# A linear-attention block and a balanced mixture of experts in one kernel: attention tiles as 64x64 products, x written behind the loads, and gathers that are issued where their lists are made

## The chip, the cores and the metric

The kernel runs on one NeuronCore of one Trainium2 chip. The metric is the device time of one execution in microseconds (us), less is better. Engines are named as the profile names them: PE is TensorE (matmuls; PEld is its weight load, which overlaps), DVE is VectorE, ACT is ScalarE, POOL is GpSimd, SP is SyncE, which here does nothing but issue DMAs. All tensors are float32.

## The reference

```
# attention, for 8 batches b and 8 heads h; seq 576, head_dim 64
kv  = einsum('bhsd,bhse->bhde', k, v)            # 64 x 64 for each head
out = einsum('bhsd,bhde->bhse', q, kv)
out = out / sqrt(mean(out*out, -1) + 1e-6) * g_norm
x   = out as (8*576, 8*64) = (4608, 512)         # a token's eight heads side by side

# mixture of experts: 8 experts, each takes exactly 4608/8 = 576 tokens
logits = x @ w_gate                              # (4608, 8)
# all 36864 logits in falling order: a token goes to the first expert that still has room
assigned = greedy_in_order(-logits, cap=576)
for e in range(8):                               # w1[e]: 512 x 1024, w2[e]: 1024 x 512
    out[assigned == e] = relu(x[assigned == e] @ w1[e]) @ w2[e]
```

## The kernel before

**Attention.** The work runs in eight slots, one for each batch. In slot `b` the kernel multiplies the tiles of batch `b` (`one`, line 464) and, between the tiles, prepares batch `b+1` (`prepare`, line 365, a generator that the slot advances by one step after each tile). Preparing a batch means: products of k and v on 64x64 quarters of the array (`sum_kv`, line 395), transposes of q (`turn_q`, line 380, into `qt`), the sum of the two halves of kv (line 417), and the gate's part: kv is transposed (line 431), copied out (`kvt`, line 433) and multiplied with `w_gate` (line 442), so that `kvx` holds for each head 64 columns of kv and 8 columns that yield the logits. A tile is 128 tokens of all 8 heads: eight products with 128 tokens as stationary columns and 72 moving columns. An even batch has four tiles; an odd one has a fifth, made of the last 64 tokens of its own and of the batch before, and that mixed tile is done as sixteen 64x64 products (line 479). Two ScalarE passes empty a tile's PSUM buffer (squares, line 485; copy to `o_sb`, line 486), VectorE sums the squares (line 490), and at the end of the slot `scale` and `logits` make the norm and the logits. GpSimd writes the normed rows to `xo` (line 511); for the last tiles (`late`) ScalarE does it instead (line 516), behind all else. Matmuls of ones (`ones`, line 361; 128x512 bf16) are put between these products: one at a slot's first tile, two at the fourth, two ahead of the kv products.

**The load queue.** All loads of q, k and v, and all writes of x to DRAM (`x_dram`), go through SP's queue in one written order, and `paced` holds each DMA until the third before it has landed. A load of batch `b+2` is issued where batch `b` has freed the buffer (`again`). The x writes wait in a list, and once it holds eight the oldest are issued at the end of a slot.

**The choice.** A chain of small DVE and PE steps (`threshold`, `assign`, `fetch`; lines 646 to 871) finds the first expert and its 576 tokens. The expert's weights are loaded, its rows of x gathered by five indirect DMAs that POOL issues (line 875), and transposed (`turn`, line 969).

**Experts.** For each expert `t`, `layers(t)` does the first layer (`one_layer`, line 1065) and the second (line 1025) by a seven-product scheme: each matrix is cut in two by two, and some of the products have a sum or difference of blocks as operand. Those sums are made on POOL: `sw` of w1's blocks (line 955, four for each of the four steps `i` of the first layer), `tw` of w2's blocks (line 1103, eight), `sh` of the hidden rows (line 1017, four after step 1 and four after the last step). The program order of POOL is kept by `in_order`: it runs its instructions in the order in which they were written. While PE works on expert `t`, the search for the next expert's tokens is fed in between (`search`, by estimated times), so that the place where the list of tokens of `t+1` (`ids`, line 869) becomes known moves from layer to layer. The gather of those rows is not put there: it waits in the list `gathers` and is written when the first layer of expert `t` has been written in full, behind the last four `sh`.

Of the kernel before, what the change touches and what calls it, by code (L numbers as in the profile page):

```python
# [7 lines left out]
FT = mybir.dt.float32  # L8
# [18 lines left out]
def kernel(  # L27
# [339 lines left out]
    def prepare(b):  # L367
# [3 lines left out]
        NT = NP * R // 2  # L371
        qt = att.tile([P, 2, NT, HP], FT, name="qt", tag="qt", bufs=3)
        turned_q[b] = qt
# [46 lines left out]

        kvx = att.tile([P, H, W], FT, name="kvx", tag="kvx", bufs=3)
        for n in range(2):
# [7 lines left out]
        for r in range(NP):  # L430
            nc.tensor.transpose(t_ps[:, r, :], kv[:, r].rearrange("p l d -> p (l d)"), ident[0:D, 0:D])
        kvt = att.tile([P, NP, D], FT, name="kvt", tag="kvt")
        nc.scalar.copy(kvt, t_ps)
        yield
# [5 lines left out]
        for r in range(NP):  # L440
            for n in range(2):
                nc.tensor.matmul(w_ps[n * D:(n + 1) * D, r], lhsT=kvt[:, r, :],
                                 rhs=gw[:, r].rearrange("p l e -> p (l e)"), start=True, stop=True)
        nc.vector.tensor_copy(kvx[:, :, D:W], w_ps.rearrange("p r (l e) -> p (r l) e", l=2))
# [3 lines left out]

    LAG = 4
    writes, late = [], []  # L450
    last_own = GC - (R + 1) // 2

    def tiles(c0, rows):
# [3 lines left out]
        o_sb = att.tile([P, T, H, W], FT, name="o_sb", tag="o_sb", bufs=2)  # L457
        xo = att.tile([P, T, H, D], FT, name="xo", tag="xo", bufs=LAG + 1)
        ms = att.tile([P, T * H], FT, name="ms", tag="ms")
# [3 lines left out]

        def one(t, copies, fill):

            o_ps = psa.tile([P, 2, 512], FT, name="o_ps", tag="o", bufs=2)
            ones(fill, o_ps[:, 0, :])
            for r2 in range(NP // 2):
                for l in range(2):
                    for rp in range(2):  # L470
                        r = 2 * r2 + rp
                        at = [slice(h * HP, (h + 1) * HP) for h in range(2)]
                        halves = rows[t]
                        parts = [(slice(0, P), halves[0], 2)] if halves[0][0] == halves[1][0] else [
                            (at[n], half, 1) for n, half in enumerate(halves)]
                        for rows_at, (bn, j), m in parts:
                            block = R * r + j
                            ks = slice(block % 2 * D, (block % 2 + 1) * D)
                            nc.tensor.matmul(  # L479
                                o_ps[rows_at, rp, (2 * r2 + l) * W:(2 * r2 + l + 1) * W],  # L480
                                lhsT=turned_q[bn][ks, l, block // 2:block // 2 + m].rearrange("p x c -> p (x c)"),
                                rhs=kv_of[bn][ks, 2 * r + l], start=True, stop=True)
            o4 = o_ps[:, :, 0:NP * W].rearrange("p b (h w) -> p b h w", w=W)
            sq = att.tile([P, H, D], FT, name="sq", tag="sq")
            nc.scalar.activation(sq.rearrange("p (b h) d -> p b h d", b=2), o4[:, :, :, 0:D], ACT.Square, scale=D ** -0.5)  # L485
            copies.append(lambda: nc.scalar.copy(o_sb[:, t].rearrange("p (b h) w -> p b (h w)", b=2), o_ps[:, :, 0:NP * W]))  # L486
            if own or t != T - 2:
                while copies:
                    copies.pop(0)()
            nc.vector.reduce_sum(out=ms[:, t * H:(t + 1) * H], in_=sq, axis=AXX)  # L490
# [38 lines left out]
    with tc.manual_schedule(engines={PE, DVE, ACTE, SPE}):  # L529
# [3 lines left out]
        for b in range(B):  # L533
# [6 lines left out]
            if b in choose_at:  # L540
                early(*choose_at[b])
            for t in range(len(rows)):
                one(t, copies, {0: 1, 3: 2}.get(t, 0))
                next(parts, None)
                if b < 2 or t == 3 or b == 6 and t == 2:
                    chore()
# [6 lines left out]
            logits()  # L553
            if b < B - 1:
                chore(2 if b == 6 else 1)

            while len(writes) >= 2 * LAG:
                writes.pop(0)()
# [245 lines left out]

    on_pool, in_second, gathers = [], set(), []

# [13 lines left out]
    def fetch(t, which, index, later):  # L820
# [50 lines left out]
        nc.vector.tensor_copy(got, s_ps[:, :, GC + 1:GC + 3])  # L871
        def gather():
            for n, (_, nr) in enumerate(blocks):
                xg = moe.tile([P, DM], FT, name="xg", tag="xg", bufs=NB)
                tokens = nc.gpsimd.indirect_dma_start(  # L875
                    out=xg[0:nr], out_offset=None, in_=x_dram,
                    in_offset=bass.IndirectOffsetOnAxis(ap=ids[0:nr, n:n + 1], axis=0))
                in_order(tokens)
                rows_of[t, n] = xg
            return tokens  # L880

        if t == 0 or t - 1 in in_second:
            tokens = gather()
        else:
            gathers.append(gather)
        if t == 0:
# [112 lines left out]
    def layers(t):  # L999
# [106 lines left out]
        yield from one_layer()  # L1106
        in_second.add(t)
        while gathers:
            gathers.pop(0)()
        for i in range(FH):  # L1110
# [138 lines left out]
```

## Time and profile before

| | us |
|---|---|
| median of 3 runs (lowest, highest) | 660.36 (658.67, 660.51) |
| the profiled execution: its own time / its span | 660.36 / 658.6 |
| attention: start of the span to the last tile's product | 0 to 121.3 |
| choice of the first expert, its loads and gather | 123 to 164 |
| experts | 164 to 657 |
| PE busy / DVE / ACT / POOL | 605.8 / 387.8 / 194.5 / 389.3 |

"Busy" sums the spans of an engine's instructions. A PE that is busy need not be at its peak: matmuls are pipelined, so that what a group of them takes is better read as the time from its start to the start of the next group. In a timeline line the first number is the start in us from the start of the span, the second the length, and a bracket at the end gives how long the engine had been idle and what ended that. In the list of waits the numbers are the total, the count, and the longest.

### The profile page before, as it was taken

The page shows a single profiled execution, that of the slowest core. Times are in us where ns is not written, and L with a number is a line of the kernel's source. Part 1 is how long each engine was busy: PE and PEld are TensorE (multiplying, and loading weights), DVE is VectorE, ACT ScalarE, POOL GpSimd, SP SyncE. Part 2 cuts the span into 40 slices and gives each one's busy share as a digit, 9 for nine tenths or more (in the row PEclk, how much of TensorE's full clock was granted, in tenths as well). Part 3 has the DMA queues.
Part 4 walks back from the last instruction along what each step waited for, and adds up shares of the span by engine and source line. Part 5 has one row for each costly group of instructions (what it writes and reads, how often), then busy time and mean ns, then how long its engine had stood idle before and what let it go on. Part 6 is the DMA issues. An engine that isn't in the chain of part 4 may idle for free.

```text
span 658.6 us, 12759 instructions
## 1 busy us (share of the span) xinstructions
PE 605.8 (92%) x4932; PEld 464.6 (71%) x4932; DVE 387.8 (59%) x1249; ACT 194.5 (30%) x395; POOL 389.3 (59%) x405
## 2 busy tenths in 40 slices
PE   7989998335899999999999999999999999999994
PEld 4767777232678677867786786778678867877873
DVE  4466667778678588668757956976671053123201
ACT  1555665611131223123212222231223123222300
POOL 1035434104585487749846974887388669848822
PEclk9999999657999999999999999999999999999998
DMA  8999989416306402710442072109103620721001
GB/s 270 310 315 295 292 291 340 154 50 199 128 0 204 164 33 71 257 41 33 158 171 73 1 262 99 41 0 323 46 32 100 229 72 1 279 84 37 0 9 64
DMA packets 49852, 91.02 MB, mean 138 GB/s; under 512 B 3712, under 2 KB 20096, under 8 KB 49792
## 3 DMA queue, kind: packets, MB, share of 16 engines
q1 hardware_dynamic: 43200, 71.31, 31.6%
q0 software_dynamic: 5888, 18.88, 8.3%
q8 instruction: 39, 0.64, 0.4%
q14 instruction: 21, 0.17, 0.1%
q10 hardware_dynamic: 704, 0.02, 0.1%
HBM read 71.32 MB, written 18.87 MB: 137 GB/s over the span
## 4 chain that ended last, share of the span: by engine, by line
PE 77%; DVE 9%; DMA 5%; issue 4%; ACT 3%; POOL 1%; POOLq 0%; SPq 0%; DVEq 0%; ACTq 0%
PE x_ps L1065 13%; PE x_ps L1025 11%; PE z_ps L1065 9%; PE y_ps L1065 9%; PE z_ps L1025 7%; PE y_ps L1025 7%; PE o_ps L479 4%; PE y_ps L1127 4%; PE kv_ps L395 3%; PE t_ps L969 3%; PE qt_ps L380 2%; DMA v_sb<-in_v_dram 2%; DMA q_sb<-in_q_dram 2%; PE given_ps L651 1%; PE given_ps L646 1%
## 5 line engine op out<-in xcount | busy, mean ns | idle before, releaser
L1070 ACT COPY h<-x_ps 128x288 f32<-128x288 f32 x93 | 37.2, 400 | 166.5 <-PE x_ps L1065 153.7
L1065 PE MATMUL x_ps<-xs,sw 128*128 128x288 f32 x248 | 71.3, 409 | 0.0
L875 POOL DMA_INDIRECT xg<-x_dram,ids x40 | 38.1, 952 | 51.8 <-DMA w_sb<-in_moe_w_dram 37.7
L992 POOL DMA_INDIRECT out_dram<-y_sb,outs x32 | 31.5, 983 | 55.8 <-DVE y_sb L1163 41.1
L1025 PE MATMUL x_ps<-tw,sh 128*128 128x256 f32 x256 | 61.6, 384 | 0.0
L972 ACT ACTIVATE xt<-t_ps,g_col 128x512 f32<-128x512 f32 (+1 forms) x40 | 25.7, 645 | 110.9 <-PE t_ps L969 110.9
L1065 PEld LDWEIGHTS x_ps<-xs,sw 128*128 128x128 f32 x248 | 46.2, 190 | 14.3 <-issue 1.7
L955 POOL TENSOR_TENSOR sw<-w_sb 128x256 f32<-128x256 f32 x64 | 46.8, 731 | 12.3 <-PE z_ps L1065 9.6
L1017 POOL TENSOR_TENSOR sh<-hid 128x512 f32<-128x512 f32 x32 | 40.7, 1272 | 19.9 <-ACT hid L1040 19.9
L1025 PEld LDWEIGHTS x_ps<-tw,sh 128*128 128x128 f32 x256 | 46.9, 190 | 7.1 <-issue 0.8
L1040 ACT ACTIVATE hid<-hid 128x576 f32<-128x576 f32 x64 | 43.8, 686 | 22.9 <-DVE hid L1079 13.1
L511 POOL TENSOR_TENSOR xo<-o_sb,inv 128x512 f32<-128x512 f32 x31 | 32.9, 1090 | 29.7 <-DVE inv L498 16.6
L1103 POOL TENSOR_TENSOR tw<-w_sb 128x512 f32<-128x512 f32 x32 | 40.1, 1276 | 5.0 <-DMA w_sb<-in_moe_w_dram 5.0
L479 PEld LDWEIGHTS o_ps<-kvx,qt 64*128 64x128 f32 (+1 forms) x640 | 33.7, 181 | 12.0 <-issue 7.1
L479 PE MATMUL o_ps<-kvx,qt 64*128 64x72 f32 (+1 forms) x640 | 38.9, 274 | 3.4 <-ACT o_sb L486 3.4
L1065 PE MATMUL z_ps<-xt,sw 128*128 128x288 f32 x128 | 37.8, 413 | 0.1
L1065 PE MATMUL z_ps<-xs,sw 128*128 128x288 f32 x128 | 37.0, 409 | 0.0
L1065 PE MATMUL x_ps<-xt,w_sb 128*128 128x288 f32 x124 | 36.8, 414 | 0.1
L1065 PE MATMUL y_ps<-xt,w_sb 128*128 128x288 f32 x128 | 36.9, 409 | 0.0
L1065 PE MATMUL y_ps<-xs,w_sb 128*128 128x288 f32 x128 | 36.7, 408 | 0.0
L490 DVE TENSOR_REDUCE ms<-sq 128x8 f32<-128x512 f32 x36 | 24.3, 683 | 20.1 <-ACT sq L485 19.8
L423 POOL COPY kvx<-kv 64x512 f32<-64x512 f32 x16 | 9.7, 607 | 43.9 <-DVE kv L417 26.9
(278 smaller groups left out, 1332.4 us busy)
## 6 DMA issues: line engine op xcount, KB each, us to landing
w_sb<-in_moe_w_dram SPq DMA_DIRECT2D x32, 512.0 KB, 5.7
w_sb<-in_moe_w_dram SPq DMA_DIRECT2D x8, 2048.0 KB, 14.3
k_sb<-in_k_dram SPq DMA_DIRECT2D x16, 576.0 KB, 5.8
v_sb<-in_v_dram SPq DMA_DIRECT2D x16, 576.0 KB, 5.8
q_sb<-in_q_dram SPq DMA_DIRECT2D x16, 576.0 KB, 6.1
x_dram<-xo SPq DMA_DIRECT2D x16, 512.0 KB, 4.4
x_dram<-xo SPq DMA_DIRECT2D x4, 256.0 KB, 4.0
xg<-x_dram,ids POOLq DMA_INDIRECT x40, 5.4
```

What stands on the lines that cost most here:

```text
L479: nc.tensor.matmul(o_ps[rows_at, rp, (2 * r2 + l) * W:(2 * r2 + l + 1) * W], lhsT=turned_q[bn][ks, l, block // 2:block // 2 + m].rearrange ...
L511: nc.gpsimd.tensor_tensor(xo[:, t], o_sb[:, t, :, 0:D], inv[:, t * H:(t + 1) * H].rearrange("p (h o) -> p h o", o=1).to_broadcast([P, H, D ...
L875: tokens = nc.gpsimd.indirect_dma_start(out=xg[0:nr], out_offset=None, in_=x_dram, in_offset=bass.IndirectOffsetOnAxis(ap=ids[0:nr, n:n + ...
L955: in_order(nc.gpsimd.tensor_tensor(o, x, y, op=op))
L992: put = nc.gpsimd.indirect_dma_start(out=out, out_offset=bass.IndirectOffsetOnAxis(ap=ids_of[t][0:nr, n:n + 1], axis=0), in_=y_sb[0:nr, :] ...
L1017: in_order(nc.gpsimd.tensor_tensor(o[:, ms], x[:, ms], y[:, ms], op=op))
L1025: nc.tensor.matmul(p_ps[:, n], lhsT=left[:, f, n * P:(n + 1) * P], rhs=right[:, f], start=first, stop=(f == FH - 1), skip_group_check=True)
L1040: nc.scalar.activation(both, both, ACT.Relu)
L1065: nc.tensor.matmul(p_ps, lhsT=lhs[:, r], rhs=rhs[:, r], start=(m in (1, 2, 4, 5) and r == 0), stop=(r == 1), skip_group_check=(m in (6, 7, ...
L1070: nc.scalar.copy(u, p_ps)
L1103: in_order(nc.gpsimd.tensor_tensor(o, x, y, op=AL.subtract))
L1127: nc.tensor.matmul(y_ps[l * nr:(l + 1) * nr], lhsT=hid[:, l * FH + f, a:a + nr], rhs=w2[:, l * FH + f, :], start=(f == 0), stop=(f == FH - 1))
```

## The change

It has two parts, in two places of the kernel.

In the attention: every tile is sixteen 64x64 products (the mixed tile's form); the mixed tile is the first of its slot and no longer the last; a slot's tiles have one matmul of ones, at the first tile; `qt` and `kvx` have two buffers in place of three, `xo` six in place of five; the gate's product is four matmuls over 128 columns in place of eight over 64, for which `kvt` is copied twice side by side; the x writes are all held back until the last load has been issued (the end of slot 4), those of batches 6 and 7 to the end; and all nine tiles of batches 6 and 7 are normed on ScalarE, in place of the last five. A step of the choice (`chore`) goes behind each tile of slot 6, and the last slots have none at their end.

In the experts: `gathers` and `in_second` are gone. The gather of the next expert's rows is written, and so takes its place in POOL's order, where `ids` is made. As the kernel is built, that is: in layer 0 behind the last four `sh`, as before; in layers 1 and 2 ahead of the last four `sh`; in layer 3 behind the third pair of `tw`, ahead of the first four `sh`; in layer 4 behind the second pair of `tw`, ahead of the last four `sw`; in layers 5 and 6 behind the first pair of `tw`, ahead of the third four `sw`.

```diff
-        qt = att.tile([P, 2, NT, HP], FT, name="qt", tag="qt", bufs=3)
+        qt = att.tile([P, 2, NT, HP], FT, name="qt", tag="qt", bufs=2)
...
-        kvx = att.tile([P, H, W], FT, name="kvx", tag="kvx", bufs=3)
+        kvx = att.tile([P, H, W], FT, name="kvx", tag="kvx", bufs=2)
...
-        kvt = att.tile([P, NP, D], FT, name="kvt", tag="kvt")
-        nc.scalar.copy(kvt, t_ps)
+        kvt = att.tile([P, NP, 2, D], FT, name="kvt", tag="kvt", bufs=1)
+        nc.scalar.copy(kvt, t_ps.rearrange("p r (o c) -> p r o c", o=1).to_broadcast([P, NP, 2, D]))
...
-            for n in range(2):
-                nc.tensor.matmul(w_ps[n * D:(n + 1) * D, r], lhsT=kvt[:, r, :],
-                                 rhs=gw[:, r].rearrange("p l e -> p (l e)"), start=True, stop=True)
+            nc.tensor.matmul(w_ps[:, r], lhsT=kvt[:, r].rearrange("p n d -> p (n d)"),
+                             rhs=gw[:, r].rearrange("p l e -> p (l e)"), start=True, stop=True)
...
-    LAG = 4
+    HELD = 6
-    last_own = GC - (R + 1) // 2
+    last_own = GC - R
-        xo = att.tile([P, T, H, D], FT, name="xo", tag="xo", bufs=LAG + 1)
+        xo = att.tile([P, T, H, D], FT, name="xo", tag="xo", bufs=HELD)
...
-                        at = [slice(h * HP, (h + 1) * HP) for h in range(2)]
-                        halves = rows[t]
-                        parts = [(slice(0, P), halves[0], 2)] if halves[0][0] == halves[1][0] else [
-                            (at[n], half, 1) for n, half in enumerate(halves)]
-                        for rows_at, (bn, j), m in parts:
+                        for n, (bn, j) in enumerate(rows[t]):
                             block = R * r + j
                             ks = slice(block % 2 * D, (block % 2 + 1) * D)
                             nc.tensor.matmul(
-                                o_ps[rows_at, rp, (2 * r2 + l) * W:(2 * r2 + l + 1) * W],
-                                lhsT=turned_q[bn][ks, l, block // 2:block // 2 + m].rearrange("p x c -> p (x c)"),
+                                o_ps[n * HP:(n + 1) * HP, rp, (2 * r2 + l) * W:(2 * r2 + l + 1) * W],
+                                lhsT=turned_q[bn][ks, l, block // 2],
                                 rhs=kv_of[bn][ks, 2 * r + l], start=True, stop=True)
...
-            for t in range(len(rows)):
-                one(t, copies, {0: 1, 3: 2}.get(t, 0))
+            order = range(len(rows)) if b % 2 == 0 else [len(rows) - 1] + list(range(len(rows) - 1))
+            for n, t in enumerate(order):
+                one(t, copies, 1 if n == 0 else 0, b + 1 == B and n == len(rows) - 2)
                 next(parts, None)
-                if b < 2 or t == 3 or b == 6 and t == 2:
+                if b < 2 or n == 3 or b == 6:
                     chore()
...
-            if b < B - 1:
-                chore(2 if b == 6 else 1)
-            while len(writes) >= 2 * LAG:
+            if b < B - 2:
+                chore()
+            while b in (B - 4, B - 3) and writes:
                 writes.pop(0)()
...
-        def gather():
-            for n, (_, nr) in enumerate(blocks):
-                xg = moe.tile([P, DM], FT, name="xg", tag="xg", bufs=NB)
-                tokens = nc.gpsimd.indirect_dma_start(...)
-                in_order(tokens)
-                rows_of[t, n] = xg
-            return tokens
-        if t == 0 or t - 1 in in_second:
-            tokens = gather()
-        else:
-            gathers.append(gather)
+        for n, (_, nr) in enumerate(blocks):
+            xg = moe.tile([P, DM], FT, name="xg", tag="xg", bufs=NB)
+            tokens = nc.gpsimd.indirect_dma_start(...)
+            in_order(tokens)
+            rows_of[t, n] = xg
...
         yield from one_layer()
-        in_second.add(t)
-        while gathers:
-            gathers.pop(0)()
```

## The prediction

> **What bounds the kernel now.** I read the page's busy shares and its DMA row first, then, for the attention, the list of SP's waits and the timelines of SP and PE, and for the experts the timelines of POOL and PE side by side.
>
> ```profile
> PE 605.8 (92%) x4932; PEld 464.6 (71%) x4932; DVE 387.8 (59%) x1249; ACT 194.5 (30%) x395; POOL 389.3 (59%) x405
> ...
> DMA  8999989416306402710442072109103620721001
> ```
>
> PE is busy nearly everywhere, but in the first seven slices (115 us, the attention) the DMA engines are full too. The stage has two bounds that lie close together. What SP waited for:
>
> ```profile
> SPq L87 <- DMA k_sb<-in_k_dram: 26.3, 16, 2.8
> ...
> SPq L87 <- DMA q_sb<-in_q_dram: 18.5, 12, 2.4
> ...
> SPq L87 <- PE o_ps L479: 1.0, 3, 0.5
> ```
>
> The loads wait for earlier loads, hardly ever for PE to free a buffer (1.6 us in all with two smaller rows). The queue at its end:
>
> ```profile
> 78.35 1.83 SPq L87 DMA_DIRECT2D q_sb<-in_q_dram  x2
> 81.90 4.52 SPq L520 DMA_DIRECT2D x_dram<-xo  x3
> 88.69 0.37 SPq L87 DMA_DIRECT2D k_sb<-in_k_dram  x1
> ...
> 95.50 1.96 SPq L87 DMA_DIRECT2D q_sb<-in_q_dram  x2
> ```
>
> Three x writes stand ahead of batch 7's loads: its first k goes out at 88.69 and not at 81.90. PE:
>
> ```profile
> 41.89 1.12 PE L479 MATMUL o_ps<-kvx,qt 64*128 64x72 f32 x16
> 42.93 0.66 PE L380 MATMUL qt_ps<-ident,q_sb 128*128 128x128 f32 x4
> ...
> 43.91 0.73 PE L479 MATMUL o_ps<-kvx,qt 64*64 64x72 f32 x32
> 44.57 0.66 PE L380 MATMUL qt_ps<-ident,q_sb 128*128 128x128 f32 x4
> ...
> 54.41 0.61 PE L361 MATMUL o_ps<-wide,ones_b 128*128 128x512 bf16 x2
> 54.95 1.12 PE L479 MATMUL o_ps<-kvx,qt 64*128 64x72 f32 x16
> ...
> 101.60 0.66 PE L380 MATMUL qt_ps<-ident,q_sb 128*128 128x128 f32 x4 [0.94 <-DMA q_sb<-in_q_dram]
> ...
> 123.07 0.87 PE L646 MATMUL given_ps<-best,over_c 128*32 128x8 bf16 x27 [1.79 <-ACT o_sb L486]
> ```
>
> From start to start a whole tile holds PE for 1.04 us and a mixed tile, the same work on 64x64 quarters, for 0.66. PE waits for batch 7's first q until 101.60, and the choice begins at 123.07. Among the experts PE has no wait of note, so any wait put there is paid in full. The place in layer 1 that the second part touches, POOL's lines, then PE's, then DVE's:
>
> ```profile
> 257.88 2.50 POOL L1103 TENSOR_TENSOR tw<-tw,w_sb 128x512 f32<-128x512 f32 x2
> 263.73 1.27 POOL L1017 TENSOR_TENSOR sh<-hid 128x512 f32<-128x512 f32 x1 [3.36 <-ACT hid L1040]
> 265.08 1.27 POOL L1017 TENSOR_TENSOR sh<-sh,hid 128x512 f32<-128x512 f32 x1
> ...
> 268.95 0.99 POOL L875 DMA_INDIRECT xg<-x_dram,ids  x1
> ```
> ```profile
> 266.45 1.03 PE L1025 MATMUL x_ps<-tw,sh 128*128 128x256 f32 x4
> ...
> 268.06 1.97 PE L1025 MATMUL x_ps<-tw,sh 128*128 128x256 f32 x8
> ```
> ```profile
> 262.33 0.16 DVE L869 SCALAR_TENSOR_TENSOR ids<-col,given_ps 128x5 int32<-128x5 f32 x1
> ```
>
> The second of the last four `sh` ends at 266.34, and PE reads its new half at 268.06. The gather, five issues or 5.96 us of POOL (209.56 to 215.52 in layer 0), stands behind.
>
> **The change, part by part.** The profiled execution took 660.36 us (span 658.6, 1.8 around it), which is the median of the three runs; the sum is made against it.
>
> *PE's work in a slot.* Four tiles at 1.04 - 0.66 = 0.38 each save 1.5 us. Two of three matmuls of ones at the tiles go: 54.41 to 54.95 is 0.54. The gate's product takes 0.65 for 16 records; eight records of twice the columns take between half of that and all of it: saving 0 to 0.33, I take 0.2. The copy `kvt` is twice as wide; 0.39 us now, 0.59 by the ScalarE row of the same 512 elements (line 386): +0.2 on the wait that an even slot has behind it. Together about 2.2 us. Slots 3 and 4 now run from 59.17 to 84.92, 25.7 us; they would need 21.3.
>
> Against the mixed tile's row stands a rule of the Trainium skill ("TensorEngine Tiling (Array Packing)", Key Properties): changing the tiling mode drains the array. The mixed tile has 128-wide transposes on both sides and shows 0.66 with such changes in it; by the same page's "up to 2x" (Theoretical Speedup) a tile would save 0.52 and a slot 2.1, an estimate which the next step makes void.
>
> *The loads.* A load goes out every 1.92 us ((70.59 - 23.08 - 1.4 of waits for PE) / 24 from batch 2's first k to batch 6's), so two batches' loads need 23.0 us, and PE's 21.3 no longer bounds: the load queue does, and about 0.85 us of a slot's saving is idle time again. With the writes behind the loads, batch 7's first k takes the place at 81.90, its first q is four loads on, 89.6, and lands 5.9 to 6.1 later: 95.6. PE's 1.6 us of late buffers go too: 94.0. Bounds: 92 (1.84 us per load, as from 70.59 to 79.81, and the two dips of 264 and 240 GB/s filled), 96.5 (no late buffer gained, 1.98 per load). I take 94.2 in place of 101.60, by the nearest row: -7.4. SP's queue then holds 15 x writes (6.8 MB; 349 to 376 GB/s in 100 to 110 us: 20 us, so until about 113) and nobody waits for these before the gather.
>
> *From that q to the choice.* Now 101.60 to 123.07, 21.5 us: 10.1 to slot 7's first matmul, 11.4 for slot 7. In slot 7 ScalarE waited 3.5 us for DVE, where two comparisons of the choice took 2.2; the change puts them into slot 6. There: 10.1 - 2.0 of PE's work, + 0.3 for kv, which now is later than the transposes ahead of it, + 0.7 because the comparisons stand ahead of the copy `kvx<-w_ps` on DVE (0.45 for the same 288 columns when POOL rests, 127.44; POOL rests there, since batch 6 is ScalarE's): 9.1. Slot 7: a tile of 0.8, then five tiles at ScalarE's pace, 1.03 for squares and copy, with one wait of DVE's sums (0.69 each, and 2.3 of batch 6's norm ahead of them): 7.2. Together 16.3, -5.2. Bounds 15 and 19. Attention: -12.6, between -15 and -9.
>
> *At no cost, and why.* `qt` and `kvx` with two buffers: batch b+1 takes the buffer of b-1, whose last reader, the mixed tile, now is first in the slot. `xo`: batch 6 reuses batch 0's, written by then. ScalarE norms 72 rows-by-head in place of 40, 0.24 us each (9.65 for 40): 17.4 us from about 112, until 129.5, last write landed by 134 (4.4 after issue). The first gather needs it 31.7 us after the choice begins (154.76 - 123.07), at 142: cover of 8 us; without it each us counts. POOL loses 4 x 1.09 us of norms; it was idle there.
>
> *The gathers.* Earlier landing gains nothing: PE waited once, 1.3 us, for `xg`, for the first expert. What counts is that 5.96 us of POOL come ahead of sums that PE needs. By layer, POOL's new times against PE's need:
> Layer 1: `ids` is there at 262.5, the gather ends at 268.6, `sh` starts there and not at 263.73; its second ends at 271.2, needed at 268.06: 3.2.
> Layer 2: the gather follows `tw` at 321.9; `sh` 327.9 for 324.60; second ends 330.6, needed 329.4: 1.2.
> Layer 3: from 376.0, pushes both groups; last second `sh` ends 392.0, needed 391.1: 0.9.
> Layer 4: from 431.05; uses POOL's idle 1.78 and 2.67; `sw` 438.6 for 439.88, `sh` 452.4 for 453.58: 0.
> Layer 5: from 486.95; the second `sw` of step 2 ends 494.5, needed 493.03: 1.5; later sums in time.
> Layer 6: likewise 552.55 for 551.15: 1.4.
> Sum 8.2. Upper end: POOL's bare delay at these sums (5.96 less its idle before them), without PE's margin: 4.9 + 3.4 + 2.8 + 1.5 + 3.3 + 3.3 = 19. Lower end 5, 0.7 less in each of the five. I take 8.2, which has both engines' own times.
>
> Sum: 660.4 - 12.6 + 8.2 = **656.0**.
>
> **Rivals.**
> *The gathers cost what POOL loses* (slower). Place: the last sums in layers 1 to 6; decides above 12.6 us. For it: POOL is at nine tenths in several slices. Against: PE's margins of 0.7 to 1.7 us are in the rows. At 19 us: 667.
> *The clock falls in the attention* (slower). The granted clock went to 0.50 at 118.6, with PE idle only since 117.06; but in 33.3 to 36.7, with 1.65 idle, it stayed at 1.0. The change takes ones away and makes PE wait longer once: slot 1 would be ready at 31.7 for a q that lands at 36.0. At half clock a mixed tile took 1.24 (120.05) for 0.66 to 0.73; a slot of 10.5 becomes 18.6, +7 over the loads' 11.5. One such slot decides: 656 + 7 = 663; two, 670.
> The skill ("TensorE: Matmul & The Clock Gate", Part 1) asks for an idle window of about 3.4 us; the fall after 1.6 speaks against so long a one. By the rule the 4.3 us wait costs one window at half clock, an estimate of 1.7 us, which the loads cover.
> *The loads get no faster.* Removing the writes brings q only to 98, as PE's 0.94 us of wait there shows that PE was nearly as late: attention -8.8, net 660. Against: PE's own 2.2 us per slot.
>
> **How the numbers follow.** Main case 0.60, own range 651 to 659; loads no faster 0.16 (658 to 662); gathers dear 0.13 (661 to 668); clock 0.11 (661 to 672). Range: 660.4 - 15 + 5 = 650.4 below; above, the loads' case and half of the dear gathers, 664. A measurement of this kernel tells 0.3%, 2 us, from no change: below 658.4 lies most of the main case and a little of the second, 0.61; within 2 us 0.16; above 0.23.
>
> **What would show it.** Right: q of batch 7 awaited until 92 to 96.5, a wait of about 1 us in every slot for q and none for ScalarE; tiles at 0.66; the choice from 108 to 113; `sh` late by 3 us in layer 1, PE waits on POOL of 5 to 11 us in all. Wrong: a clock under 1.0 before 100 us, tiles over 0.8, PE waiting on POOL over 12 us, or the first gather waiting for an x write.

## The result, and the profile after

| | before | after |
|---|---|---|
| median (lowest to highest), 4 runs each | 660.43 us (658.67 to 662.64) | 680.44 us (677.5 to 682.37) |
| profiled execution: own time / span | 660.36 / 658.6 | 682.37 / 680.5 |
| start of the choice of the first expert | 123.07 | 133.72 |
| from there to the end of the span | 535.5 | 546.8 |

The changed kernel is slower: ratio 1.0297, 95% interval 1.0249 to 1.0346. The forecast was 656.0 (650 to 664), so it has the wrong sign and the range does not hold the time. (The ratios leave out executions that took over 1.5% longer than the fastest of their kernel; the medians hold all of them, so the two need not agree to the last digit.)

Half of the loss, 10.65 us, is there when the choice begins, where 12.6 us had been expected as gain. The other 11.3 us came behind that point; the choice itself is 0.27 us longer. PE's busy tenths and the granted clock in tenths (the share of its full speed at which PE was clocked), in 40 slices of the span, before:

```profile
PE   7989998335899999999999999999999999999994
...
PEclk9999999657999999999999999999999999999998
```

The same rows of the changed kernel, with the DMA engines' busy share and the queue that brings the instructions (pieces, MB, share of the engines' time):

```profile
span 680.5 us, 13663 instructions
...
PE   7686979634899999799999999999999999999994
...
PEclk9888878855999999899999999999999999999998
DMA  8999678234503610801171063227022522611001
...
q8 instruction: 42, 0.69, 0.4%
```

In the first seven slices, the attention, PE's digits fell from 7 to 9 (one 7, all others 8 or 9) to as low as 6, and the clock from 9 throughout to mostly 8. What PE waited for in the whole span (total in us, count, longest):

```profile
PE o_ps L474 <- issue: 10.3, 5, 4.3
...
PE x_ps L1014 <- POOL sh L1006: 5.8, 3, 3.7
PE kv_ps L395 <- issue: 5.0, 4, 2.6
...
PE x_ps L1054 <- POOL sw L944: 2.9, 2, 1.5
...
PE qt_ps L380 <- DMA q_sb<-in_q_dram: 1.4, 1, 1.4
```

Three readings. The waits for POOL's sums, 5.8 + 2.9 = 8.7 us, are the price of the early gathers. The wait for q, which the forecast had in every slot, is there once, in the first batch, so the loads of q did not bound PE. And there is a wait that no part of the forecast has: 15.3 us in nine places in which a tile's or a kv product stood ready and waited for nothing that the profile shows. The longest, in PE's timeline:

```profile
57.31 0.73 PE L474 MATMUL o_ps<-kvx,qt 64*64 64x72 f32 x32
57.86 1.28 PE L395 MATMUL kv_ps<-v_sb,k_sb 64*64 64x64 f32 x70
58.93 0.29 PE L474 MATMUL o_ps<-kvx,qt 64*64 64x72 f32 x2
58.97 0.23 PE L395 MATMUL kv_ps<-v_sb,k_sb 64*64 64x64 f32 x2
59.03 0.49 PE L474 MATMUL o_ps<-kvx,qt 64*64 64x72 f32 x15
63.80 0.65 PE L474 MATMUL o_ps<-kvx,qt 64*64 64x72 f32 x15 [4.28 <-issue]
```

The stall is in the middle of a tile: 17 of 32 records, 4.28 us of nothing, 15 more. The profile names no operand that was missing. Until then PE had gone through 64x64 products (a tile, the kv products, half a tile) as one unbroken run, at some 55 matmul records in a microsecond (a float32 product has two of them). The trace's DMA records give the reason: the instructions themselves come in by DMA, in pieces of 16384 bytes, and each of the nine stalls ends 1.30 to 1.56 us after such a piece. The three longest:

```
changed kernel, start of the piece + its length = end | PE goes on | later by
28.71 + 0.92 = 29.63 | 31.04 | 1.41
61.30 + 1.04 = 62.34 | 63.80 | 1.46
87.22 + 0.97 = 88.19 | 89.75 | 1.56
```

PE had used up the instructions that it held and waited for the next piece. The counts say so too. The 42 pieces for 2 x 5364 records (matmuls and weight loads) are 64 bytes for each record, so a piece holds 256 of them, or 128 matmul records with their weight loads. From one of the nine stalls to the next PE ran 127, 254, 127, 128, 126, 509, 381 and 381 matmul records, which is one, two, three or four pieces each time: PE stops where a piece ends, whatever instruction stands there.

The clock followed. Windows of PE's timeline, in each: us, PE busy, granted clock, DMA share, GB/s:

```profile
60.55:63.96 3.41, 0.16 (x9) 1.00 0.97 346
63.96:74.20 10.24, 9.25 (x109) 0.50 0.76 261
94.68:98.10 3.42, 2.62 (x27) 1.00 0.86 282
98.10:101.51 3.41, 3.15 (x37) 0.50 0.99 341
```

The stall at 60 us leaves 3.4 us nearly empty, and behind it PE runs at half clock for 10.24 us. The second pair is a different fall: 2.62 of 3.42 us were busy, with q's transposes, the gate's products and the gaps between them. In all the clock was 0.5 for 34.1 us ahead of the choice: 23.9 behind three of the stalls, 10.2 (three times 3.41) behind such stretches, beside which the kernel before has two products of ones.

### The profile page after: what moved, and what is told of

Same layout as the page of the kernel before. It is cut to its first block, busy times and chain, and to the rows that moved or that the text cites. A ratio compares the mean times of both kernels' runs of the same rounds, so it can differ in the third digit from the quotient of the medians.

```text
span 680.5 us, 13663 instructions
## 1 busy us (share of the span) xinstructions
PE 607.5 (89%) x5364; PEld 464.5 (68%) x5364; DVE 384.6 (57%) x1249; ACT 204.0 (30%) x427; POOL 384.5 (57%) x401
## 4 chain that ended last, share of the span: by engine, by line
PE 67%; POOL 10%; DVE 9%; issue 7%; DMA 3%; ACT 2%; POOLq 0%; SPq 0%; DVEq 0%; ACTq 0%
PE x_ps L1054 10%; PE x_ps L1014 10%; PE z_ps L1014 7%; PE z_ps L1054 7%; PE y_ps L1054 7%; PE y_ps L1014 6%; PE y_ps L1113 4%; PE o_ps L474 4%; POOL xg L870 3%; PE qt_ps L380 3%; POOL sh L1006 3%; PE kv_ps L395 3%; PE t_ps L958 3%; DMA v_sb<-in_v_dram 2%; POOL tw L1092 1%
## 5 line engine op out<-in xcount | busy, mean ns | idle before, releaser
L1014 PE MATMUL x_ps<-tw,sh 128*128 128x256 f32 x256 | 63.7, 393 | 5.8 <-POOL sh L1006 5.8
L1054 PEld LDWEIGHTS x_ps<-xs,sw 128*128 128x128 f32 x248 | 46.1, 190 | 17.9 <-POOL sw L944 3.9
L961 ACT ACTIVATE xt<-t_ps,g_col 128x512 f32<-128x512 f32 (+1 forms) x40 | 25.7, 644 | 105.0 <-PE t_ps L958 105.0
L1029 ACT ACTIVATE hid<-hid 128x576 f32<-128x576 f32 x64 | 43.8, 686 | 23.2 <-DVE hid L1068 13.1
L506 POOL TENSOR_TENSOR xo<-o_sb,inv 128x512 f32<-128x512 f32 x27 | 28.7, 1090 | 37.0 <-DVE inv L493 37.0
L474 PE MATMUL o_ps<-kvx,qt 64*64 64x72 f32 x1152 | 32.3, 250 | 11.3 <-issue 10.3
L474 PEld LDWEIGHTS o_ps<-kvx,qt 64*64 64x64 f32 x1152 | 25.8, 151 | 19.1 <-issue 17.3
L1143 ACT COPY u<-x_ps 128x512 f32<-128x512 f32 x24 | 14.0, 582 | 74.2 <-PE x_ps L1014 65.9
```

What stands on the lines that cost most here:

```text
L474: nc.tensor.matmul(o_ps[n * HP:(n + 1) * HP, rp, (2 * r2 + l) * W:(2 * r2 + l + 1) * W], lhsT=turned_q[bn][ks, l, block // 2], rhs=kv_of[b ...
L506: nc.gpsimd.tensor_tensor(xo[:, t], o_sb[:, t, :, 0:D], inv[:, t * H:(t + 1) * H].rearrange("p (h o) -> p h o", o=1).to_broadcast([P, H, D ...
L1014: nc.tensor.matmul(p_ps[:, n], lhsT=left[:, f, n * P:(n + 1) * P], rhs=right[:, f], start=first, stop=(f == FH - 1), skip_group_check=True)
L1029: nc.scalar.activation(both, both, ACT.Relu)
L1054: nc.tensor.matmul(p_ps, lhsT=lhs[:, r], rhs=rhs[:, r], start=(m in (1, 2, 4, 5) and r == 0), stop=(r == 1), skip_group_check=(m in (6, 7, ...
```

## Experiments

The expectations name four theories. F: runs of 64x64 products use the instructions up faster than they are fetched. C: the missing ones let the clock fall; later C1 (the ones) and C2 (the gate's wider products). W: the late writes are to blame. And the gathers: 8 to 9 us of waits, whatever the attention does.

**Each part alone.** The kernel before with only its gathers issued where the lists are made:

```diff
-        def gather(): ...
-        if t == 0 or t - 1 in in_second: ...
+        for n, (_, nr) in enumerate(blocks): ...   # as in the change
```

> The kernel before with the gathers part of the change alone. In the changed kernel's trace PE waits 8.7 us for POOL's sums in layers 1 to 6, and the clock falls once for one window of 3.4 us (at 282 us), where the longest of these waits was. If the two parts add, this run has the 11 us that the experts took longer: 669 to 672, the choice begins at 123 as before, and PE waits for POOL 8 to 9 us. If the clock's fall there was handed on from the attention, 668 at most and no fall.

Measured: 672.66 us median of 4, ratio 1.019 (1.0107 to 1.0272); profiled 669.35. PE's waits:

```profile
PE x_ps L1018 <- POOL sh L1010: 5.8, 3, 3.7
...
PE x_ps L1058 <- POOL sw L948: 3.0, 2, 1.5
```

The same waits, 8.8 us, with the attention as it was (choice at 120.96), and once a fall of the clock for 3.4 us right behind the longest of them (269.94 to 273.36; in the changed kernel 282.42 to 285.83), so that fall was not handed on from the attention. The gathers' part is what the forecast had, a little more by the clock.

The changed kernel with the late gathers of before, so that the attention's part is alone:

> The changed kernel with the gathers put back behind the first layer: the attention part alone. If the parts add: the choice begins at about 134, the total is 669 to 673, PE has 15 us of waits named issue in the attention, and no wait for POOL. If the attention's loss came from POOL's or the gathers' side, about 650.

Measured: 665.55 us median of 10, ratio 1.0064 (1.0027 to 1.0101); profiled 665.79, choice at 128.56, 11.2 us of issue waits in eight places, each of which ends 1.35 to 1.52 us behind a piece:

```profile
PE kv_ps L395 <- issue: 6.0, 4, 3.9
PE o_ps L474 <- issue: 5.2, 4, 3.1
```

The loss is smaller than expected, and it varies: the same attention began the choice at 133.72 in the changed kernel. The two ratios' excesses, 1.9% and 0.6%, add to 2.5%, the lower end of the interval of 2.97%.

**The tiles.** That last kernel with its tiles as 128-column products, as before the change (few ones, four gate products and the writes behind the loads stay):

```diff
-   for n, (bn, j) in enumerate(rows[t]): ... lhsT=turned_q[bn][ks, l, block // 2]
+   for rows_at, (bn, j), m in parts: ...     lhsT=turned_q[bn][ks, l, block // 2:block // 2 + m]
```

> The attention part alone, but tiles as eight products of 128 columns again (the mixed tile stays at 64x64); still few ones, writes behind the loads, four gate products. Theory F (PE runs out of instructions: the quarter products use up the instructions of a fetched piece faster than the next piece comes): PE's waits named issue fall under 3 us in the attention, and the choice begins by 118. Theory C (the clock falls because ones are missing): the clock falls in the attention as often as in e2, and the choice begins at 125 or later. Theory W (the late writes are to blame): nothing changes against e2, 134.

Measured: 664.04 median of 10, ratio 0.9978 (0.993 to 1.0027); choice at 123.66. Issue waits fell from 11.2 us to 0.5: that is F's share. W, by which nothing was to change, is out. But the choice did not come at 118, and the clock still fell: four times, from 31.97, 59.27, 86.58 and 113.89 us on, the first three for 3.4 us, one for every two slots. PE ahead of the first of them, and the windows:

```profile
28.28 0.66 PE L380 MATMUL qt_ps<-ident,q_sb 128*128 128x128 f32 x4
28.87 0.46 PE L431 MATMUL t_ps<-ident,kv 64*128 64x64 f32 x4
30.07 0.66 PE L380 MATMUL qt_ps<-ident,q_sb 128*128 128x128 f32 x4 [0.74 <-ACT kvt L433]
30.56 0.96 PE L441 MATMUL w_ps<-gw,kvt 128*128 128x16 f32 x8
31.84 0.61 PE L380 MATMUL qt_ps<-ident,q_sb 128*128 128x128 f32 x2 [0.32 <-DVE kvx L443]
```
```profile
28.55:31.97 3.42, 2.36 (x21) 1.00 0.95 329
31.97:35.38 3.41, 3.41 (x53) 0.50 0.88 280
```

PE was busy for 2.36 of 3.42 us, with transposes and gate products alone, and lost the clock.

The converse, the kernel before with nothing but its tiles changed (three ones at the tiles of a slot, eight gate products, writes between the loads, late gathers):

> The kernel before with nothing changed but the tiles, as 64x64 products (all products of ones, eight gate products, writes between the loads, late gathers). Theory F (short products use up the instructions faster than they are fetched): waits of PE put down to issue of 3 to 11 us in the runs of tiles and kv products, choice at 121 to 129 us, time 660 to 668. Theory C alone (only the missing ones lower the clock): no such waits beyond 1 us, clock at 1.0 until 115 us, choice at 119 to 121, time 656 to 659.

Measured: 669.35 median of 4, ratio 1.0117 (1.0039 to 1.0195); profiled 669.48, choice at 132.1. PE's waits and one place in its timeline:

```profile
PE kv_ps L395 <- issue: 8.2, 5, 3.3
PE o_ps L475 <- issue: 5.2, 7, 2.0
```
```profile
54.52 1.21 PE L395 MATMUL kv_ps<-v_sb,k_sb 64*64 64x64 f32 x62
59.03 0.39 PE L395 MATMUL kv_ps<-v_sb,k_sb 64*64 64x64 f32 x10 [3.31 <-issue]
```

This is F by itself, and more of it than F had expected (3 to 11 us): 13.4 us of issue waits, with every product of ones in place. (12.3 us of them end 1.25 to 1.61 us behind a piece. Three of 0.36 us are no waits: a product of ones stands there whose record is missing from the trace, while that of its weight load is there.) The form of the tiles, which was to save 1.5 us of each slot, makes the kernel slower. The stall ends 1.25 us behind a piece of instructions (56.72 + 1.06 = 57.78), and the clock fell behind it (59.9 to 70.1).

Half of it, 64x64 products in the first and third tile only:

```diff
-   if halves[0][0] == halves[1][0] else [
+   if t % 2 and halves[0][0] == halves[1][0] else [
```

> The kernel before with 64x64 products only in the first and third tile of each slot, the second and fourth in 128-column products. F: half as many more instructions, in shorter runs, so the waits put down to issue are 1 to 6 us (13.4 to 13.6 us with all tiles so), choice at 122 to 127 us, time 660 to 666. If it is the 64x64 products themselves (a change of form on the array, some price of each): the waits are half of it, about 7 us, in as many places, choice at 126 to 128, time 664 to 666. If short tiles are a gain where they do not starve: choice at 119 to 121, time 656 to 659.

Measured: 666.87 median of 6, ratio 1.0078 (1.0039 to 1.0118); choice at 126.7. Issue waits of 2.4 us in three places, not half of 13.4: the stalls grow faster than the count of short products, as for a supply that runs dry, and not as for a price of each product. The time is above what 2.4 us explain; in the profiled run, the fastest of the six, PE also waited 2.7 us for q at 33 us, with 6.8 us of half clock behind it, and a second fall of 10.2 us behind the 1.71 us stall at 82 us.

**What makes the instructions late.** The changed attention (late gathers) with the loads of batches 2 to 7 left out; these batches compute on the data of the first two:

```diff
-            if b + 2 < B:
-                for name in names:
-                    load(name, b + 2, h)
...
-   ([loaded.pop((name, b, h)) for h in range(2)] for name in "kvq")
+   ([loaded[name, b % 2, h] for h in range(2)] for name in "kvq")
```

> The attention of the change with 64x64 tiles and late gathers, its batches from the third on computed from the loads of the first two: the loads of batches 2 to 7 are left out, the rest is all there. If the instructions come late because the DMA engines are full of loads, the waits of PE put down to issue fall from 11.2 us to under 3 us in the attention and the instruction pieces take well under 0.9 us each; if a piece comes late by its own time (about 1 us of transfer and 1.4 us more until PE goes on), the waits stay at 7 us or more.

Measured: 655.15 us, one run; choice at 117.9.

```profile
PE o_ps L472 <- issue: 2.7, 5, 1.2
PE kv_ps L395 <- issue: 0.8, 1, 0.8
PE kv_ps L361 <- issue: 0.3, 1, 0.3
```

By these rows the waits went from 11.2 to 3.8 us. Of the 3.8 only 2.4 are waits, three of them (1.18, 0.79 and 0.41 us), which end 1.26 to 1.42 us behind a piece; the other four, of 0.33 to 0.36 us, stand where the record of a product of ones is missing (36 of 45 are there, and all 45 weight loads). So 2.4 us, under the 3 that were expected if the loads are the cause. The pieces did not get faster: 21 of them took 1.08 us on average (0.99 with the loads).

What did get shorter is the time until a piece starts. Counting records as above gives the time at which PE began on a piece; the transfer of the next piece began 2.1 us later on average in the changed kernel (18 pieces, at most 4.8), 2.0 us in the kernel with late gathers, and 1.0 us here. These are estimates, good to some tenths of a us. So the loads are shown to be behind most of the stalls, by a later start and not by a slower transfer; what holds the start up, for instance load packets ahead of the piece on a DMA engine, is an inference, since no record shows the moment at which a piece is asked for.

One more thing can be read from this run: without loads and without a stall two slots take 23.9 us (first kv product to first kv product, 61.8 to 85.7), where 21.3 had been forecast for PE. PE was at half clock for 3.4 us of it; at full clock it would have been some 22.2, an estimate.

The other way round, more time for each instruction, with two products of ones ahead of every tile:

```diff
-   one(t, copies, 1 if n == 0 else 0, ...)
+   one(t, copies, 2, ...)
```

> The attention of the change with 64x64 tiles and late gathers, with two products of ones ahead of every tile in place of one ahead of the first of a slot: 16 more products in two slots, at 0.22 to 0.27 us each 3.5 to 4.3 us, some 14 to 17 us over the attention. Theory F (the 64x64 runs use the instructions up faster than they come while the loads fill the DMA engines): the ones, few instructions that take long, give the fetch time, so the waits put down to issue fall from 11.2 us to under 4 us; with the clock up as well the choice begins at 127 to 132 us, time 663 to 669. If the pace doesn't matter: the waits stay at 8 us or more, choice at 137 or later, time 672 or more.

Measured: 667.27 median of 6, ratio 1.0086 (1.0045 to 1.0128); choice at 132.6.

```profile
PE o_ps L361 <- issue: 2.2, 1, 2.2
PE kv_ps L395 <- issue: 2.0, 2, 1.3
PE o_ps L474 <- issue: 1.7, 2, 1.1
```

5.9 us lie between the two expectations (under 4, 8 or more), so this run does not decide. It points to pace, but the same attention without these ones had 15.3 us in one trace and 11.2 in another. Ones ahead of a tile do not reach the long runs inside (kv products between two tiles), and the choice began 4 us later than without them.

**The clock, the ones and the gate's products.** Three neighbours of the kernel with 128-column tiles. First with the two ones of the fourth tile back (`{0: 1, 3: 2}.get(n, 0)`):

> The attention of the change with tiles of 128 columns as before (the run above: 664.04, choice at 123.66 us, clock down for 3.4 us at 32, 59, 87 and 114 us), and with the two products of ones of the fourth tile put back. Theory C1 (the clock falls because the ones are gone from the stretch of transposes and gate products): no fall before the tail, choice begins at 120 to 121 us, time 657 to 660. Rival C2 (it falls because the four 128-column gate products leave PE idle where the eight of 64 columns did not): the falls stay, choice at 123 to 124, time 661 to 665.

Measured: 663.63 median of 10, ratio 1.0047 (1.0012 to 1.0083); profiled 660.03, choice at 122.1, one fall of the clock (85.9 to 89.3) where there had been four. The profiled run is the fastest of the ten; the median lies in the range of C2, and the kernel did not become faster. Second, without these ones but with the eight gate products of before:

```diff
-   kvt = att.tile([P, NP, 2, D], ...); nc.tensor.matmul(w_ps[:, r], lhsT=kvt[:, r] (128 columns), ...)
+   kvt = att.tile([P, NP, D], ...);    for n in range(2): nc.tensor.matmul(w_ps[n*D:(n+1)*D, r], lhsT=kvt[:, r, :], ...)
```

> The same kernel without the ones of the fourth tile, but with the eight gate products of 64 columns as before. C1: the clock falls stay (three or four of 3.4 us ahead of 115 us), choice at 123 to 124, time 661 to 665. C2: no fall before the tail, the gate products take 0.65 us again in place of 0.96, choice at 119 to 121, time 656 to 660.

Measured: 661.66 median of 10, ratio 0.9964 (0.9911 to 1.0018); profiled 657.82, choice at 120.4. This median lies in the range of C1, the profiled run in that of C2. PE in the stretch that is to be compared, the same kernel's window over it, and the windows of its one fall:

```profile
86.27 0.66 PE L380 MATMUL qt_ps<-ident,q_sb 128*128 128x128 f32 x4 [0.52 <-ACT kvt L433]
86.85 0.65 PE L442 MATMUL w_ps<-gw,kvt 128*64 128x16 f32 x16
87.60 0.44 PE L380 MATMUL qt_ps<-ident,q_sb 128*128 128x128 f32 x2
```
```profile
84.24:87.65 3.41, 2.79 (x39) 1.00 0.88 306
33.04:36.45 3.41, 0.92 (x39) 1.00 0.89 293
36.45:43.28 6.83, 6.83 (x85) 0.50 0.95 315
```

No fall behind this stretch, without any ones in it; the only one (36.5 to 46.7) is behind a wait of 2.49 us for batch 2's q. So in the profiled runs neither C1 nor C2 alone: with four gate products and no ones every second slot's stretch lost the clock, with either change undone one did or none.

The other runs bear this out only in part. The mean granted clock of every run is on record; twice what it lacks to 1, times the span, is the time at half clock (an estimate; some 38 to 44 us of it belong to the choice and the end, which all kernels have). Medians over the runs that the ratios use: 57.9 us with four gate products and no ones at the fourth tile (47 to 65), 53.5 with these ones back (42 to 67), 53.9 with the eight gate products back (46 to 65), and 44.7 with both back, in the third kernel below (38 to 58); the kernel before has 44.8 (42 to 60). So with both back the clock holds as before, while what either does alone is lost in the spread. The ones also cost time of their own: 16 of them at 0.27 us are 4.3 us, an estimate, which may be why the kernel with the ones back gained nothing.

The four products of 128 columns, which were to save 0.2 us, cost: 0.96 for 0.65, and the waits for the twice as wide `kvt` and for `kvx` around them are 0.74 + 0.32 for 0.52. What exactly the clock's control counts stays open: in the first of these kernels one window with 2.67 us busy lost the clock (82.50 to 85.91) and another with 2.67 (27.89 to 31.30) kept it.

Third, both back, that is the kernel before with only the order changed (writes behind the loads, mixed tile first, two buffers, nine tiles on ScalarE, steps of the choice earlier):

> The kernel before with the order part alone: writes behind the loads, mixed tile first, two buffers of qt and kvx, nine tiles normed on ScalarE, the choice's steps earlier; tiles of 128 columns, all ones, eight gate products and the late gathers as before. F and C: no new waits, clock at 1.0 until the attention's end, PE bounds its slots at 12.7 us, q of batch 7 is there before PE needs it (100.5), and slot 7 without DVE's comparisons is 4 us shorter: the choice begins at 116 to 119, total 652 to 657. W: slower than before, the x writes being awaited by the first gather.

Measured: 660.33 median of 10, ratio 0.9973 (0.9933 to 1.0012), choice at 127.7 in a profiled run that at 667.53 is the slowest of the ten (3.17 us of waiting for batch 2's q, and half clock behind it). F and C had promised 652 to 657 with the choice at 116 to 119, W a kernel slower than before; neither came. The second of the three kernels shows why, in SP's queue and in PE's timeline:

```profile
88.24 3.25 SPq L87 DMA_DIRECT2D q_sb<-in_q_dram  x2
92.07 36.48 SPq L520 DMA_DIRECT2D x_dram<-xo  x17
```
```profile
102.16 0.80 PE L395 MATMUL kv_ps<-v_sb,k_sb 64*64 64x64 f32 x36
102.89 0.66 PE L380 MATMUL qt_ps<-ident,q_sb 128*128 128x128 f32 x4
...
120.37 0.87 PE L647 MATMUL given_ps<-best,over_c 128*32 128x8 bf16 x27 [1.77 <-ACT o_sb L486]
```

The last q went out at 88.24 in place of 95.50, 7.3 us earlier, and PE read it at 102.89 without a wait, later than before (101.60). PE was the bound: two slots take 24.6 us (77.6 to 102.2), against 25.7 before, which is the two slots' ones. From q to the choice it is 17.5 us for 21.5: that part of the order did pay 4 us.

**A version that beats both.** The kernel of the last two fences, with eight ones in batch 2 ahead of the transposes that waited for q:

```diff
+            if b == 2 and r == 0:
+                ones(8)
```

> The run with 128-column tiles, eight gate products and one product of ones in a slot, writes behind the loads and late gathers (661.66 us median, its profiled run 657.82 with the choice at 120.4 us), and eight products of ones in the third batch just ahead of its first transposes, where PE waited 2.5 us for q and the clock then was down for 6.8 us. Clock theory: no fall there, choice at 116.5 to 118.5 us, time 653 to 658, ratio 0.988 to 0.996. If the fall is not that window's: choice at 120 to 121, ratio 0.995 to 1.000.

Measured: 656.32 median of 6 (653.85 to 658.77), ratio 0.9914 (0.988 to 0.9948). The ratio is the one expected, the early choice was not seen: the profiled run is the slowest of the six, and though the clock did hold at 36 us, it had fallen at 19 us for 13.7 us, so the choice came at 121.6:

```profile
15.56:18.97 3.41, 2.62 (x33) 1.00 0.96 320
18.97:32.63 13.66, 13.66 (x206) 0.50 0.92 317
```

That window holds the first batch's transposes and gate products. Four more ones there:

```diff
+        if b == 0:
+            ones(4)
         turn_q(3)
```

> The run before it (656.32 us, ratio 0.9914, its profiled run 658.77 with the clock down from 19.0 to 32.6 us and the choice at 121.6 us) with four more products of ones in the first batch, ahead of its fourth group of transposes, where PE waits for a copy. Its clock fell right after a stretch of 3.4 us that held transposes, gate products and 0.77 of busy time. Clock theory: no fall from 19 us on, choice at 114 to 118 us, time 652 to 656, ratio 0.985 to 0.993. If ones in such a stretch don't decide: the fall stays in the profiled run, choice at 120 to 122, ratio 0.990 to 0.996.

Measured: 656.03 median of 12 (652.98 to 672.75), ratio 0.9919 (0.988 to 0.9959), the same within the intervals. In the profiled run (659.03) both places kept the clock, and it fell in a third, 82.4 to 89.3, behind a stall for instructions of 1.5 us, with the choice at 119.6. Where the clock falls is not the same in each run, and which of the two additions the gain owes what is not shown. Both kernels are 0.8% faster than the kernel before, with intervals clear of 1; without the additions it was 0.4%, with an interval that holds 1. These intervals overlap, so the gain by the additions is not shown by the times; the time at half clock, reckoned as above, is 43.9 and 43.2 us (38 to 54) for 53.9 (46 to 65) without them.

## Why the prediction was wrong, by its own steps

*PE's work in a slot* (forecast -2.2 us a slot) failed, and is the main cause. The tiles did take what the mixed tile's row promised, 0.55 to 0.74 us from start to start. But that row stands alone in its slot, between transposes; sixteen short products for every eight, tile after tile with the kv products between, are a run that uses instructions faster than they came: 15.3 us of stalls, and 23.9 us at half clock behind three of them. The tiles alone cost 1.2% (0.4 to 2.0%). The step added up durations of instructions and never asked for the instructions as a resource. The trace of before had the row for it in the page's list of queues:

```profile
q8 instruction: 39, 0.64, 0.4%
```

Those are 39 pieces of 16384 bytes; the change added 432 matmul records with as many weight loads, all in the attention. The Trainium skill has the mechanism ("Runtime: NRT & Kernel Launch", Instruction fetch mechanics): refills in blocks of 16 KiB, with a boundary's cost "mostly hidden". The size is what these traces show, 16384 bytes; that it is hidden holds for the kernel before, and not here, where a boundary cost up to 4.28 us.

Two smaller terms of the step had the wrong sign, or may have had it. The gate's product in four parts was taken at -0.2: it measured +0.31, and more by the wait around it. The products of ones were taken as time saved, 0.54 a slot: in the profiled run with the gate's products as changed, the clock fell in every second slot without them, but putting them back gained no time.

*The loads* (-7.4): half right. The queue did get that much earlier where PE let it (88.24 for 95.50, in the kernel with 128-column tiles). It bounds only a PE that needs less than 23.0 us for two slots, and no measured one did: 24.6 with the whole tiles, and 23.9 with 64x64 tiles and no loads at all (some 22.2 at full clock). In the changed kernel the last q went out at 96.66, late because PE freed the buffers late (SP waited 12.9 us for kv products and 4.1 for transposes of q, for 1.6 in all before), and nothing waited for it.

*From that q to the choice* (16.3 us forecast): 17.9 in the changed kernel (115.78 to 133.72, with one stall of 1.14 and 3.4 us of half clock in it), 17.5 with whole tiles. This step held.

*At no cost*: held. The lists of waits show none for one of the two buffers or of `xo` to come free; ScalarE's norms took 17 us (133.8 to 150.7; 17.4 forecast), and from the start of the choice to the first transposes of the gathered rows (171.77) it is 38.05 us, for 37.78 before.

*The gathers* (+8.2, 3.2 of it in layer 1): waits of 8.7 us; layer by layer 3.71, 1.10, 0.99, none, 1.48 and 1.47 for 3.2, 1.2, 0.9, 0, 1.5 and 1.4. The step held in its mechanism and not only in its sum; not in it was the clock, down for 3.4 us behind the layer 1 wait. From the choice on, 11.3 us were lost, of which 8.7 are these waits, at most 1.7 that fall and 0.3 the choice; 0.6 stay open.

Of the rivals, "the clock falls in the attention" (661 to 672, chance 0.11) named an event that came. Its price was too small and its cause another: it looked for one long wait for q, and the falls came behind stalls for instructions and behind busy stretches. The rule of the Trainium skill weighed there, an idle window of about 3.4 us ("TensorE: Matmul & The Clock Gate", Part 1), was rightly doubted, but the doubt was not carried on: if 1.6 us of idle time can do it, so can gaps that were there all along, once the ones beside them go. The runs show falls behind windows with 2.36, 2.62, 2.67 and 2.77 of 3.4 us busy, while one of 1.76 (33.29 to 36.70 in the kernel before) passed.

The sum: forecast -12.6 + 8.2, measured +10.65 + 11.3. Of the 23.2 us missed in the attention, 15.3 are stalls; PE was busy in about 30 of the 34.1 us at half clock, and what it did there would have taken half as long at full clock, so these cost up to 15 us, an estimate from the windows; part of both took the place of the waits for loads that the forecast had in each slot.

## What to carry to other kernels

A duration from the trace is the price of an instruction in its surroundings; before multiplying it, ask what the new run of them consumes that the old one did not, the instruction stream too. Splitting matmuls into quarters doubles the instructions for the same work: where they form long runs beside full DMA queues, look for waits in the middle of a tile that nothing explains, and compare them with the instruction transfers. Here a piece took about 2.1 us until its transfer began, 1.1 us for the transfer and 1.4 us until PE went on, 4.6 us in all (an estimate from the changed kernel's means), while 64x64 products used up its 128 matmul records in 2.3 us: such a run has to be broken up by longer products.

Fillers that look like waste may hold the clock, and they cost time of their own. Take them out one place at a time, look at the granted clock behind each place, and judge from several runs, since the windows fall differently in each.

## What the runs showed of the hardware

PE's instructions came in pieces of 16384 bytes, one for each 126 to 128 matmul records with their weight loads; a piece took 0.88 to 2.1 us. In the attention of every run a stall of more than 0.4 us that the profile puts down to issue ended 1.25 to 1.62 us after the end of a piece. With the loads' traffic such stalls summed to 11.2 to 15.3 us in 64x64 tiles, without it to 2.4.

The granted clock fell to 0.50 for 3.41 us or a multiple of it, in the attention up to 13.66, and not only behind idle time: also behind windows that were 69 to 81% busy, when these held transposes and short products.

Four float32 products of 128 stationary by 16 moving columns took 0.96 us; eight of 64 stationary columns, the same work, took 0.65.
